# A new listed order of all steps for a fused decay attention and mixture-of-experts attention kernel

## The chip, the cores and the metric

The kernel runs on one core of one Trainium2 chip. The metric is the device time of one execution in microseconds (us); lower is better. Engines are named as the profile names them: PE is TensorE's matmul, PEld its weight load, DVE is VectorE, ACT is ScalarE, POOL is GpSimd, and SP is the queue from which all data transfers (DMAs) are issued.

## The reference

Two layers on a batch of 8, 576 positions, 8 heads of 64. The first is causal attention whose scores get a decay made from a running sum of log(f); the second is a mixture of 4 attention experts of 64 columns, of which each position takes the best 2.

```
scores = q @ k.T / 8 + cum[:, None] - cum[None, :]      # cum = cumsum(log(clip(f)))
attn   = softmax(causal(scores)) @ v                    # 8 batches, 8 heads
x      = attn, heads side by side                       # [8, 576, 512]
for e in range(4):
    ye  = softmax(causal((x @ wq[e]) @ (x @ wk[e]).T / 8)) @ (x @ wv[e]) @ wo[e]
    out += (e among the best 2 of x @ w_gate) * its weight * ye
```

## The kernel before

**Units.** The work is cut into 48 units of two heads (or two experts) each: `a0_0` to `a0_3` are the four pairs of heads of batch 0, `m0_0` and `m0_1` the two pairs of experts of batch 0, and so on. Each unit goes through the same tasks. `prep` loads or computes queries and keys and splits them into a rounded part and a rest (L386, L389, L401 on ACT, L399 on DVE, for three early units on POOL; L544 on PE for experts). `max` finds the row maxima: matmuls into PSUM (L618), reductions by DVE (L624, L640, L673, L680), a transpose on PE (L685), a copy on ACT (L688), and a small DMA into the key tile (L376). `scores` makes the scores (L716, L717 on PE) and their exponentials (L734 to L770 on ACT), and then lets POOL work: it cuts the diagonal blocks (L703, two at a time, 128 partitions; L772 for the last 64 rows, 64 partitions) and sums the probabilities by columns (L776, L778, L780 on 128 partitions, L782 on 64). `attend` multiplies by the values (L801). For each pair of units `rows` sums the rows on PE (L839), transposes the result on DVE (L854, twice), adds a constant (L857, 128x18 elements), takes the reciprocal (L859), spreads it (L865 on ACT, L868 on DVE) and sends it round by DMA (L874); `apply` scales the outputs with it (L886, L905, L913). Experts have a `front` as well (values and gate: L439, then many small DVE operations, L473 to L505, and L512) and an `out` (L936, L940, and the output DMAs, L943 and L946).

**What sets the order.** Each task is a Python generator that yields after every step of a few instructions. `ORDER` lists 4939 steps, two digits of base 64 for each: the task's number. Each time a number comes, that task goes on to its next yield. So `0a` is `rows a0_1`, `0f` is `scores a0_2`, `0k` is `scores a0_3`, `0q` is `max a1_0`, `0v` is `max a1_1`, `0t` is `prep a1_1`, and `4w` is the task that keeps PE warm with 110 matmuls on zeros (L205) during the start. At the end of the function every instruction is chained behind the one before it on its own engine, so each engine runs its instructions exactly in the listed order, and one that waits holds up all behind it on that engine. `SLOTS` says for each new tile which buffer it takes: three for the probabilities (`P`), eight PSUM banks (`banks`), five wide tiles, twenty strips, and so on. ORDER and SLOTS were written by a replay of the whole program outside the kernel, which is not part of the source.

Of the kernel before, what the change touches and what calls it, by code (L numbers as in the profile page):

```python
# [37 lines left out]
0C0C0C0C0F0v0k0v0F0F0r0r0w0w0w0w0r0l0w0m0m0s0m0w0w0b4A0m4A0m0b0C0m0b0w0m0b0w0w0w0b0b0H0H4y0b0A0w0w0w0m0H0H0m0C0C
0C0C0w0w0w0w0w0C0O0w0M0H0b0H0H0n0H0H0R0s0s0H0n0n4A0n0n0N0N0N0R0R0n0n0H0H0H0n0n0H0w0R0H0H0H0w0M0M0N0H0H0H0H0H0H0H
0H0N0N0R0N0N0N0N0A0N0A0w0M0M0Y0w0R0R0w0N0N0N0N0N0N0N0N0N0N0N0N0N0N0N0N0N0N0N0N0N0N0N0N0O0N0r0D0D0D0D0D0D0D0O0O0O  # L40
0O0O0D0D0r0r0r0D0D0D0D0H0H0O0O0O0O0D0D0u0F0D0D0D0O0O0H0H0O0O0O0O0O0O0O0M0Y0w0F0D0Y0O0F0Y0x0x0x0O0O0D0D4A0y0y0I0y
0O0O0y0y0O0Y0S0I0I0I0I0I0I0I0I0I0I0I0I0I0I0I0I0I0Y0I0y0O0N0N0+0R0n0+0+0+0+0+0+0D0D0D0D0D0y0R0R0I0I0+0+0+0O4A0O0O
# [40 lines left out]
323230302X2X2X2X2X2X2X2X2X30303030303030303030322C323232302X322S322C31312N2I2X2S2I2N2N2I2C3c2C2C2X2X2X2T2T2T2T2T
2T2T2T2T2T2T30323030302T2T322T2T2T2T2C32323232323032322C2C31312T2O2O2W3c2O322O3c353535352Y2Y2Y2Y2O2T2T3230322T32
2R2Y2Y2Y2Y2Y2Y2Y2Y2Y2Y2Y2Y3c3c3c352Y2Y2Y2Y323232322Y2O3c353535353d2C322C2O3h2T2T2T353535353535353535362T3535353e
3e3535353535353e3e3e3e3e3e3e35353535353535353535333333362U36362U2U2Y362Y2Y322Y2Y36363636363h363e2O2O333330303030
# [957 lines left out]
```

## Time and profile before

| | us |
|---|---|
| median of 3 runs | 648.0 |
| the three runs | 646.73, 648.0, 650.79 |
| the profiled execution | 649.53 |
| its span, first to last instruction | 647.8 |
| PE busy in the span | 632.1 |
| DVE busy | 554.8 |
| ACT busy | 480.0 |
| POOL busy | 408.3 |

The profiled execution took 1.7 us more than its span, and 1.5 us more than the median of the three runs. Matmuls overlap in the records, so that busy time on PE says that matmuls were under way, not how densely they followed each other.

### The profile page before, as it was taken

Reading aid. Unit: us, or ns where it says so; the run is one execution under the profiler, and the core shown is the slowest. Engines: PE = TensorE matmul, PEld = TensorE weight load, DVE = VectorE, ACT = ScalarE, POOL = GpSimd, SP = SyncE. Lnnn points to the kernel's source line nnn. Section 1 sums busy time; section 2 is a strip of 40 time slices with the busy share of each in tenths; the row PEclk is TensorE's granted clock in tenths of the full one; section 3 lists DMA queues with packets and bytes.
Section 4 is the critical chain, followed back from the end, with each engine's and each line's share of the span. In section 5 each row is a group of like instructions: output and inputs, shape, how many; then the busy total and the mean of one; then the engine's idle time right before and its main releaser. Section 6 shows DMA issues by size and latency. Waiting matters only on the chain.

```text
span 647.8 us, 15136 instructions
## 1 busy us (share of the span) xinstructions
PE 632.1 (98%) x5303; PEld 539.5 (83%) x5303; DVE 554.8 (86%) x1541; ACT 480.0 (74%) x1057; POOL 408.3 (63%) x519
## 2 busy tenths in 40 slices
...
GB/s 201 168 141 155 91 79 165 116 135 87 157 88 125 136 71 155 113 131 77 93 184 86 152 122 94 142 74 131 168 95 83 191 98 58 80 92 69 60 83 203
DMA packets 33531, 76.90 MB, mean 119 GB/s; under 512 B 4395, under 2 KB 4875, under 8 KB 33455
## 3 DMA queue, kind: packets, MB, share of 16 engines
...
q14 instruction: 34, 0.28, 0.1%
...
## 4 chain that ended last, share of the span: by engine, by line
PE 93%; DVE 4%; DMA 1%; issue 1%; ACT 0%; POOL 0%; ACTq 0%; DVEq 0%
PE pp_m L544 16%; PE ob_a L801 10%; PE s_a L717 7%; PE s_a L716 7%; PE m_a L618 7%; PE po L936 7%; PE pv L439 7%; PE ob_m L801 5%; PE m_m L618 4%; PE s_m L717 4%; PE s_m L716 4%; PE oa_a L801 4%; PE sm_a L839 3%; PE warm L205 2%; PE oa_m L801 2%; PE sm_m L839 1%
## 5 line engine op out<-in xcount | busy, mean ns | idle before, releaser
L703 POOL TENSOR_SCALAR_AFFINE_SELECT P_a<-P_a 128x256 f32<-128x256 f32 x128 | 65.7, 530 | 102.6 <-ACT P_a L734 61.7
L716 PE MATMUL s_a<-ka_a 128*128 128x320 f32 (+4 forms) x384 | 104.3, 296 | 0.0
L717 PE MATMUL s_a<-kq 128*128 128x320 f32 (+4 forms) x384 | 102.5, 294 | 1.6 <-DMA kq<-ms_a 1.6
L624 DVE CUSTOM_DVE_ANT_0 junk_a<-m_a,mask 128x192 bf16<-128x192 f32 (+2 forms) x186 | 86.8, 484 | 15.1 <-PE m_a L618 12.5
L618 PE MATMUL m_a<-kq 128*128 128x448 f32 (+3 forms) x372 | 78.6, 306 | 6.1 <-DVE mxs_a L624 4.8
L552 ACT ACTIVATE kq<-pp_m 64x288 fp32r<-64x288 f32 x128 | 51.7, 404 | 33.0 <-PE pp_m L544 31.7
L717 PEld LDWEIGHTS s_a<-kq 128*128 128x128 f32 (+1 forms) x384 | 68.6, 180 | 3.6 <-DMA kq<-ms_a 2.4
L716 PEld LDWEIGHTS s_a<-ka_a 128*128 128x128 f32 (+1 forms) x384 | 69.2, 180 | 2.9 <-issue 0.9
L557 DVE TENSOR_TENSOR ka_m<-pp_m,kq 64x288 fp32r<-64x288 f32 x128 | 58.2, 455 | 12.9 <-ACT kq L552 10.7
L776 POOL TENSOR_TENSOR R_a<-P_a 128x896 f32<-128x896 f32 x32 | 68.5, 2144 | 0.0
L801 PE MATMUL ob_a<-P_a,va 128*64 128x320 f32 (+1 forms) x512 | 68.5, 410 | 0.0
L618 PEld LDWEIGHTS m_a<-kq 128*128 128x128 f32 x372 | 57.6, 180 | 11.5 <-DVE mxs_a L624 6.2
L703 POOL TENSOR_SCALAR_AFFINE_SELECT P_m<-P_m 128x256 f32<-128x256 f32 x64 | 30.5, 492 | 56.8 <-ACT P_m L734 43.4
L801 PEld LDWEIGHTS ob_a<-P_a,va 128*64 128x64 f32 x512 | 36.3, 139 | 24.6 <-issue 1.0
L778 POOL TENSOR_TENSOR R_a<-R_a,P_a 128x640 f32<-128x640 f32 x32 | 53.9, 1685 | 1.6
L716 PE MATMUL s_m<-ka_m 128*128 128x192 f32 (+3 forms) x192 | 51.3, 293 | 0.0
L717 PE MATMUL s_m<-kq 128*128 128x192 f32 (+3 forms) x192 | 50.3, 294 | 0.0
L624 DVE CUSTOM_DVE_ANT_0 junk_m<-m_m,mask 128x448 bf16<-128x448 f32 (+2 forms) x96 | 44.9, 483 | 6.0 <-PE m_m L618 5.0
L399 DVE TENSOR_TENSOR ka_a<-xin_a,ka_a 64x1152 fp32r<-64x1152 f32 x32 | 46.6, 1457 | 0.9 <-ACT ka_a L389 0.2
L399 DVE TENSOR_TENSOR ka_a<-xin_a,kq 64x1152 fp32r<-64x1152 f32 x29 | 42.8, 1475 | 0.7
L734 ACT ACTIVATE P_a<-s_a 128x512 f32<-128x512 f32 x64 | 35.8, 595 | 5.8 <-PE s_a L717 5.5
L386 ACT ACTIVATE kq<-xin_a 64x1152 fp32r<-64x1152 f32 x32 | 37.1, 1158 | 3.5 <-DMA xin_a<-in_qk_dram 3.2
...
## 6 DMA issues: line engine op xcount, KB each, us to landing
...
```

Source lines behind the costliest of these rows:

```text
L399: eng.tensor_tensor(lo, x[at], hi.bitcast(F32), ALU.subtract)
L544: nc.tensor.matmul(pp[:, :HS], w[:, c, es], x[c][:, gs], start=(n == 0), stop=(n == 3 * KC - 1))
L552: nc.scalar.activation(hv[h], src[h], AF.Copy)
L557: nc.vector.tensor_tensor(lo[:, h, gs], src[h], hv[h].bitcast(F32), ALU.subtract)
L618: nc.tensor.matmul(dst, qB[0:K, h, i0 : i0 + dst.shape[0]], kB[0:K, h, j0:j1], start=True, stop=True)
L624: nc.vector.tensor_tensor_reduce(jk[:, :n], src, mask[:, MW - n :], 1.0, init, ALU.add, ALU.max, acc)
L703: return nc.gpsimd.affine_select(pv, pv, [[0, 2], [1, 128]], ALU.is_ge, 0.0, base=0, channel_multiplier=-1)
L716: nc.tensor.matmul(dst, kaf[:, c : c + m], qA[:, h, i0:i1], start=True, stop=False)
L717: nc.tensor.matmul(dst, kqf[0:K, c + h * S : c + h * S + m], qB[0:K, h, i0:i1], start=False, stop=True)
L776: g.tensor_tensor(r[:, :, 128:S], p[:, :, 320:768], p[:, :, 768:1216], ALU.add)
L778: g.tensor_tensor(r[:, :, 256:S], r[:, :, 256:S], p[:, :, 1216:1536], ALU.add)
L801: mm = nc.tensor.matmul(dst[64 * h : 64 * h + 64, c0 : c0 + rhs.shape[-1]], vs[h][0:kp, blk], rhs, start=first, stop=last,)
```

## The change

ORDER and SLOTS are replaced; no instruction is added, removed or altered. Both lists hold the same 4939 steps, each task as often as before, and give 4311 PE instructions, 1157 on DVE, 1055 on ACT, 514 on POOL and 378 DMAs, as before. (The profile counts some more: a matmul on plain fp32 is two there, and a reduction with an accumulator read is two.) The scores and the row sums of the units come in the same order as before; in `max` one pair of neighbours and in `attend` six pairs change places. There are 110 warming matmuls as before, of which some now stand a little later. The new lists come from a replay in which POOL's operations on 64 partitions can keep DVE off the shared port for a whole run of POOL operations. Of the 104 lines of ORDER and the changed lines of SLOTS these matter for the text: the lines around `rows a0_1` (the fourth `0a` is L857, the fifth L859) and, as a sample, the slots of the probabilities and wide tiles.

```diff
 ORDER = """
...
-0q0q0q0q0q0q0q0q0f0f0f080k0q0q0k0t0k080k0q0q0q0q0k0q030f0k0q0q0f0q0q080q0q0q0t0t0A0k0k0f0k0k0k0k0k0o0q0q0a0t090k
-0q0q0q0q0q0k0k0a0k0v0k0k0f0v0v0v0v0v0v0v0f4A0a0v0v0v0k0k0a0g0A0A0v0F0a0v0v0v0r0v0a0a0v0r0r0r0k0r0r0A0v0v0v0v0v0v
...
+0q0j0j0q0f0f0f0f0q0q0t0q0k0k0k0A0q0k0q0d0f0f0q0k0t0k0k0k0a0t0t0k0a0a0a0a0f0q0F040k0k0k0q0k0q0k0f0k0q0q0f0k0q0i0k
+0k0q0q4A0q0q0q0k0k0k0k0k0f0q0v0v0v0v0v0v0f0v0v0v0v0p0v0A0k0q0A0a0A0F0a0g0v0v0v0v0v0v4A0v0v0g0t0k0q0o0v0l0v0q0l0a
...
 SLOTS = """
-P 01201201201202102102102010210210201201210212012012
-wide 01234234102314023410231042230142104214302142032041320123012431243124013421304123041
...
+P 01201201201021021021012010210120120120102101201021
+wide 01234243120423102143021430123401324014320143014302143210324102410340213420314203142
...
```

## Rows read from the trace of the kernel before

**Rows 1.** The page: busy time by engine, share of the span, instructions
```profile
PE 632.1 (98%) x5303; PEld 539.5 (83%) x5303; DVE 554.8 (86%) x1541; ACT 480.0 (74%) x1057; POOL 408.3 (63%) x519
```

**Rows 2.** The page: the chain that ended last, by engine
```profile
PE 93%; DVE 4%; DMA 1%; issue 1%; ACT 0%; POOL 0%; ACTq 0%; DVEq 0%
```

**Rows 3.** Stretches: length, busy by engine (instructions), granted clock, DMA share, GB/s
```profile
0.00:20.00 20.00, 16.78 (x123) 13.34 (x124) 13.77 (x33) 15.49 (x19) 18.56 (x29) 1.00 0.65 213
...
40.00:60.00 20.00, 17.46 (x148) 13.68 (x146) 18.76 (x45) 15.29 (x31) 17.75 (x21) 1.00 0.51 140
...
400.00:500.00 100.00, 100.00 (x853) 85.89 (x855) 86.73 (x248) 77.59 (x173) 64.97 (x86) 1.00 0.46 120
```

**Rows 4.** Waits of PE: total us, times, longest us
```profile
PE m_a L618 <- DVE mxs_a L624: 4.8, 5, 2.8
PE mp_a L600 <- DVE mxs_a L597: 2.1, 2, 1.2
PE s_a L717 <- DMA kq<-ms_a: 1.6, 3, 0.8
...
PE m_a L618 <- DMA kq<-ex: 0.7, 1, 0.7
PE mp_a L685 <- DVE mxs_a L624: 0.7, 1, 0.7
```

**Rows 5.** Timeline of DVE, 54 to 61 us: start, length, instruction
```profile
54.86 5.05 DVE L857 TENSOR_SCALAR rc_a<-zt_a 128x18 f32<-128x18 f32 x1
```

**Rows 6.** Line 857: lengths as min/median/max ns
```profile
L857 DVE TENSOR_SCALAR rc_a<-zt_a x16: 160/178/5053, 54.9 to 573.6; 128x18 f32<-128x18 f32 x16
```

**Rows 7.** Timeline of POOL in the same stretch
```profile
54.35 0.76 POOL L703 TENSOR_SCALAR_AFFINE_SELECT P_a<-P_a 128x256 f32<-128x256 f32 x2
55.06 0.28 POOL L772 TENSOR_SCALAR_AFFINE_SELECT pl<-pl 64x128 f32<-64x128 f32 x1
55.33 1.56 POOL L778 TENSOR_TENSOR R_a<-R_a,P_a 128x640 f32<-128x640 f32 x1
56.85 2.08 POOL L776 TENSOR_TENSOR R_a<-P_a 128x896 f32<-128x896 f32 x1
58.89 0.98 POOL L780 TENSOR_TENSOR R_a<-R_a,P_a 128x384 f32<-128x384 f32 x1
```

**Rows 8.** Timeline of PE, 60.5 us on; in brackets its idle time before
```profile
60.58 0.41 PE L618 MATMUL m_a<-kq 128*128 128x320 f32 x1 [2.77 <-DVE mxs_a L624]
```

**Rows 9.** Chain that ended last: start us, us, what; 61 to 97 us
```profile
61.17 1.54 PE oa_a L801 x8
62.71 2.98 PE ob_a L801 x20
...
94.91 0.80 PE oa_a L801 x8
95.71 2.06 PE ob_a L801 x20
```

**Rows 10.** A stretch behind the wait, columns as in rows 3
```profile
62.00:64.00 2.00, 2.00 (x12) 1.22 (x10) 1.90 (x9) 1.73 (x4) 0.00 (x0) 0.50 0.48 93
```

**Rows 11.** Timelines of DVE and POOL: two other long DVE operations
```profile
154.42 2.13 DVE L857 TENSOR_SCALAR rc_m<-zt_m 128x18 f32<-128x18 f32 x1
...
151.16 5.36 POOL L776 TENSOR_TENSOR R_a<-P_a 128x896 f32<-128x896 f32 x2
156.48 1.57 POOL L778 TENSOR_TENSOR R_a<-R_a,P_a 128x640 f32<-128x640 f32 x1
...
182.95 3.21 DVE L473 TENSOR_TENSOR g<-vm 128x80 f32<-128x80 f32 x1
...
181.24 0.29 POOL L772 TENSOR_SCALAR_AFFINE_SELECT pl<-pl 64x128 f32<-64x128 f32 x1
181.50 2.10 POOL L776 TENSOR_TENSOR R_a<-P_a 128x896 f32<-128x896 f32 x1
...
184.52 1.54 POOL L778 TENSOR_TENSOR R_a<-R_a,P_a 128x640 f32<-128x640 f32 x1
```

More of the change, by code (lines that the diff above doesn't have):

```diff
@@ L38 @@
[L38 to L42, printed above, removed]
@@ L83 @@
[L83 to L86, printed above, removed]
-33333333333333333333333333333333363e2D3636362P363e3e3e363636332D2D332P363636362T3h2D363e2Z353e3e363e3e3e3636363c
@@ new lines @@
+4w4w4w4w4w4w4w4w4w4w4w4A4x050000000500000202020202020c02020207024w024w4w4w4w4w0207074z02020202060202020202024A4A
+020c4w020202020207074w4w4w4w054w4w4w074z0c024w03034w070707074w054w0702020707074y0707074w4w4w4w070c0c0c0c03030707
+034w050303030e03070h03030303034z030303030707074z4z074z4z0303030303070707070e0e0e0h0e0e0e0e0e0e0h0j040e0e0c0c0e0e
+0e0e0e0e4z0e080303080h080e0e0e080808080h08080808080h08080h0e080e0e0j0j0j0o0t040e0j0j0j0e0e080808080808084w4w080e
+0j0j0o0o0j0j0j0j0j0j0j0j0j0j0j0j0j0j0j0j0e0j0o0h0f0f0f0f0o0f0f0o0o0q0f09080j0t0j090f0f080f0f0f0f03080q0A0q0f0q0q
@@ new lines @@
+0r0n0H0H0b0A0M0H0N0N0R0R0A0Y0N0N0N0N0u0M0N0N0N0N0N0N0N0N0N0N0N0N0N0N0N0N0N0N0N0N0N0N0N0O0N0D0M0D0R0D0D0O0O0O0D0N
+0r0O0O0r0O0M0M0O0O0D0D0D0D0O0D0N0H0D0D0O0O0D0D0O0D0D0D0O0O0G0F0O0O0O0D0H0H0O0w0r0w0D0H0F0F0x0H0N0D0D0D0Y0x0O4y0y
+0b0+0y0M4A0I0Y0Y0Y0Y0I0I0I0O0O0N0O0M0M0O0I0I0I0I0O0I0I0I0I0I0I0I0I0I0y0I0I0I0I0I0I0I0y0y0y0R0Y0O0O0O0O0R0R0R0R0R
+0R0R0R0R0R0R110R0D0R0R0R0R0R0M0R0R0R0R0R0R0R0R0R0R0P0P0P0P0M0M0D0R0S0S0+0+0+0+0+0S0S0S0+0P0P0M0P0R0S0S0S0+0P0S0P
+0P0P0P0S0+0S0y0P0Z0M0M0M0M0M0S0S0S0S0S0I0I0D0P0P0P0S0S0P0S0S0S0S0P0P0P0y0P0+0+0M0M0M0M0M0S0D0S0S0M11110M0M0M0+0+
@@ new lines @@
+0+0+0+0+0+0+180+0+0+0R0S0S180+0+11110S0+0K0z0K0z0K0J0K0K0M0M0M0S0S0Y0M0M0+0E0E0M0J0J0x0+0E0y0P0P0P0P0T0+0z1d130M
+0z0M0M0M0T0T0T0T0T0T0T0T0T0T0+11111313130+13130T0T0T130T0T131313130T1a0T0Q13130T0T0T1313131813130-0-0T130T0T180K
+0-0-1313131813130Q0Q0T0-0-0-0-0-0-0-13130P0K0-190-0K0-0-0-0-1a0z0z0z1a1a0T0M1a1a1a1a1a1a0K1k0-0-0-0-0z131313131d
+1a110U0U0U180L0L180-100z1a0L1d4A4A1a1a1a1a1a0L140L0L14141a1a1k140L181a14141f1a1a1a1a1a0M1l1l0M0M140L141a0M1l0M14
+14141l141a140L141m0V0M0M1a100M0M141k141d1d1d141f14140V1k141a1a1k1b141p0V1f1b1b1k1f0V0V1f1f1f0V1f1f1b1b1b1l1l1l1l
@@ new lines @@
+101l1l1f1b1f1l1l14141414141l1l1l1l1b1l1b1b1b1b1b1b1l1w1l1b1d1f4A1f4A1l1l0-0-0-1f1f1f1f1f1l1l1l1f1f1f1f1f0-1l1l1l
+1f1f1l1l1l1l1b1b0V1l1l1l1l1l1p1p1f1p4A1p1k1k4y1m1d1b1f1m1m1m1m1m1m1m1m121f0z0z0V1k1f0L0L1f1e1m1p1p1p1p1p1p1p1p1p
+1p1p1p1p1p1p1p1b1b1b1b1b1p1p1b4A1p1p1p1p1p1p1p1p1p1p1l1g1p1m1m1m1m1m1p1p1b1g1q0V0V1g1m1m1m1g1m16161g1q161q1q1q1g
+1g1g1k1l1m1k1k1p1q1q1q1q1q161q1k1k1g1g1g1g1g1g1g161g1g1m161q1w1q1q1q1k1k1k1q1q0W1m1m1m1B1q1q1q1q1q1q1q1g1g1g1g1q
+0W161w1w1w1g1B1q1w1w1w1b151c0W0W161g1m1c1h0W0W0W0W1m1m1m1m1q1q1k1k1k1k1p1k151y1c1517171g1y1y1h1k1k1k1k1k1y1y1y1y
@@ new lines @@
+1y1y1y1k1k1k1n1g1n1n1n1n1n1g1n1y1n1n1n1n1y1h1y1y1y1n1n1n1n1n1y1y1y1y1n1n1i1B1n171k1q1r1i1i1i1n1n1q1k1I1r1N1r1r1k
+1n1k1k1k1k1k1k1B1r1r1r1r1r1r1r1r1r1r1r1r1r1r1r1r1r1r1r1I1n1o1i1i1B1B1B0W1y1y1I1I1B1I1D0X1y1y1D1D1D1D1D1D1D1D1D1D
+0X1y1716170X0X1y0X0X1y1N0X0X0X1i171o1D1o1D1D1D1D1D1D1D0X1D1y1K1n0X0X1D1D1y1D1D1D1K1y1D1y171i171s1s1k1D1n1n1D1r1K
+1K1K1z1z4y1z1z1K1K1D1K1K1K1K1D1z1P1z1z1z1z1z1z1j1z1i1K1s1z1z1K1K1K1K1K1K1K1k1j1k0X1k1k1z1r1z1r1z1E1j1z1N1V1K1E1N
+1k1E1E1j1j1j1j1E171k1E0X1t1K1K1t1N1t1j1k1j1U1K1I1E1E1E1E1E1E1E1E1E1V1V1E1U1K1K1K1U1U1U240W1U0X1E1E1K1V1I1N1N1V1K
@@ new lines @@
+1z1z1V1z1V1z1I1V1V1V1E1K1j1V1K1V1V1k1E1E1E1k1z1j1V1E1P1V1P1P1P1V1V1V1V1V1V1V1V1V1E1V1V1V1V1V1V1V1V1V1V1L1L1L1L1L
+1L1N1C1P1Z1U1P1P1P1P1U1U1P1U1U1L1L1L1L1L1W1E1E1P1P1P1t1P1P1L1L1P1P1P1L1L1L1z1L1W1P1L1W1t1z1Z1t1P1P1P1z1L1L1L1L1Z
+1Z1Z1t1t1t1t1L1Z1W1J1Z1Z1Z1L1Z1L1W1W1W1W1W1W1L1U1Z1P1P1P171V1W1Z1Z1Z1Z1Z1V1Z1Z1Z1Z1Z1Z1Z1Z1Z1Z1Z1Z1Z171Z1Z1Z1Z1Z
+1x1V1W1W0W2g1Z241P1P1G1G1G1G1F1G1Z1A1G1W1G1P1A1u1P1u1F1G1u1O1+1u1A1Q1Q1Z1Q1Q1Q1Q1u1+1Z1u1u1W1W1U1Q1Q1Q1Q1U1Q1Q1Q
+1Q1H1Q1Q1+1u1W1W1+1+1Q1U1W1+1Q1Q1W1Q1Q1+1+1Q1Q1Q1Q1+1+1U1U1U1U1U1U1U1U1+1W1F1+1W1W1W1W1W1G29291+1+1+1v1+1+1+1+1V
@@ new lines @@
+241+1+1W1W1+1+24241+1+1M24241M1u1u1u1+1H1R1R1U1W1H241W1Q1S1S1S1S1R1+1+1+1H26262626261X1X1X261S1+1X1X261X1S1H1H1v
+1H1H1v1v26261U1M251S1X2b1U1U26261U1U1X1U1U1U1X1X1X1X2626261X1X1X1U1U2h1S1U1X1X26262626261H262626261S1X1X2626261v
+1-1-1-1-1v1v1U1X291v1U1T1U1U2g1X1-1-1v1X1-1-1v1-1-1-1-1-1-1-2929291-1-1-1-1-1Y2g261T1-262b2b29291Y1Y2l1-1v2g2g2b
+1T1T1T1T2s2s1T1T2b2l2b2b2i2b2b2b202b1-1T1-1-2i2i2026262s2b1U2i2b271v27272i1X271H1U1U1-2727272b2b2b2b2b2b2i2b2i1v
+1v2i2b2b2s272i27272i1X1X1v1v1v2s2i1v271X2727272i1U2b2b2i2i2i272i2b2b2i1v27272i2i272b2b1U1U2l2i2i2a2i2b212b1U1U1U
@@ new lines @@
+2s2s2s2s2727272s2s2c2n2i2c1U2c2c2c2c2c2c2l2l2l2s2c2c2c2c2t2t2t2t2c2s2s2s2c2c1v2c2c2n2c2t212g2c2c2121212n212i2c2l
+212c2c2n2n2n2n2n2n27272n2n2l2i212c2c21212s2s2s2t2t2t2t2t2t2t2t2t2t2t2t2t2t2t2t2t2t2t2t2t2t2t2t2t2t2t2i2n2n2n2s27
+2t2t2n2s2n272x2n2n2n202n2c1H2i271v2s2i222n2u2n2n2n2n2n222222222828281T2d2d2t2i2i2g2t2g2m2e2n2222222e2e2e1T2s2u2u
+2n2e2s2E2s2j2j2j2j2j2j2u2u2J2n2u2u2u2s2u2u2u2e2j2s2s2s2s2j2j2j2j2j2j2j2s2e2u2d222s2u2s2n2u2u2u2u2u2o2o2o2o2o2o2j
+2e2j2u2j2j2u2j2u2u2u2u2E2s2E2o2j2o2u2o2u2o2o2o2s2s2o2o2f2f2j2j2E2E2o2o2o2o2E2u2Q2s2s2s2u2f2s2s2o2o2o2s2o2x2s2t2E
@@ new lines @@
+2u2x2x2x2x2o2o2o2o2x2x2x2x2x2x2x2x2x2x2x2x2x2x2x2x2x2x2x2x2x2x2x2x2x2x2x2x2x2x2f2f2f2t222G2G2G2e2G2G2G2k2k2y2y2y
+2x2x2y2y2y2y2y2y2G2G2G2y2y2k2u2p2G2s2p2j2G2y2y2j2j2y2y2y2y2y2J2E2y2v2y2y2v2v2v2j2y2v2v2y2y2y2v2v2v2v2v2v2y2v2v2G
+2v2v2v2v2v2v2v2v2v2v2v2s2s2v2R2G2y2G2y2G2G2G2G2G2G2G2G2y2y2q2G2q2w2G2q2J2q2q2w2q2G2Q2s2q2z2G2J2z2z2z2z2z2z2z2z2z
+2z2z2z2z2z2J2L2z2z2L2q2w2z2z2z2z2G2J2G2f2f2L2J2G2z2z2z2z2G232L2L232L2p2L232323232323232q2L2L2L2L2Q2z232H2L2L2L2L
+2L2L2H2L2L2H2H2L2H2Q2H2r2L232L2V2r2r2H2H2H2H2H2H2H2r2L2L2L2L2r2H2H2r2r2H2H2H2f2A2B2r2r2B2H2f2f2K2H2s2J2L2A2A2L2Q
@@ new lines @@
+2s2S302L2B302Q2Q2B2B2s2B302V2V30232H30302S2S2S3030302S2S2S232H2M2M2M2H2H2X30232S2L232S2S2S2V2M2M2M2F2H2V2M2M2S2S
+2S2S2S302M2M2S2S2S2S2S2S2B2B30302M302Q3h2M2S2S2M2M2M2M2M30302X302S2B2S2X2X2X312X2X2X2M2S2S2X2M2S31312X3131312V35
+302V312X2V31313131313c3130312M2M3131313131223030312M2M2C2T2T2X302M2M2M312S312X31322r2r2X2T2H312X2X2X313131313131
+322X31312X31302T2X2X2T2X2T2T2X2X2X322T30302T2X3132303032322T303030302T2T2T2B2T3032313230302C303030302T2C302T3232
+2T2X2T3c312X3c2X302I302C2C302C31312N2O2C322T2N2I322O2T2T322X2I323e32323232322Y323c2Y2O32322Y2Y2Y2Y2T2T2T2Y2O2Y35
@@ new lines @@
+3c2Y2Y32324y3e323e352Y2Y2Y2Y2Y3e322Y2Y2O2O3e3e2Y2Y2Y2Y2Y2Y2Y32323c2C4y3235353c353535353535352Y353535352Y35353535
+35353535353535353532353h2T3e3e353e3e35352O2N3e332O2U35353o352C2C303333332C30303e3e333e2U3c36363636363636362U2D36
+2O3e333333333e3333362D362D35333333332T36353636363636363e3e3e3333362W36332D333333333336303e3e3e3e3h3h3h36363e3636
+2P2+302Z303e3e30363636363h2Z363t2P3o34343e37372+2+2+2+2+3e2P2P3j343e3737373737373737373737373737373e3j3h3p2+2+2+
+2P373o3o373j3j3j3j33333j33372Z2P2D2D2D2D2D37373j3j3q3j3f373f3f3f3f3f3f3f3f3f3f3f3j2-2P3j3j3j3j3j3j2-3j3j3j3j383o
@@ new lines @@
+0X3j2-3j3j3j3h3q3q2P3f3q383q2-3q3q3q3q3j3q3q3f3f2P3f3f3f2D2D3q3q3i383737373f2-2P3B2-3q3q3q3q3q3q3q3f3f393j2-3t3B
+3t3j3B3q2-3B3q3q3A3A3A2-3A3j3A2D3j3k3k3k3k3k3k3k3k3k3k3k3k3k3k3k3t3t2-3o3t3o3k3A3A3A3q3A3A3v3v3q3A3v3v3v393q3k3f
+3f3v3k3q3o3B3k3k3k3B3k3B3B3k3v3v3A3A3C3F3F3F3q2P393q3q3B3B3B3B3B3B3B3B3B3B3B3B3v39393v3B3B3B3B3B3B3B3B3B3B3B3B3B
+3B3B393r3B3B3C3r3r2-3B3r3C3r3k3A3A3A3C3C3C3C3C3C2D3C3f3A3v3r3r3r3r3r3F3C3r3r3r3r3r3C3A3v3v3v3v3r3r3v3M3C3A233d3A
+3C3C3C3C3v3v3k3f3f3v3C3C3r3r3k3C3v3r3r3A3t3r3r3r3v3r3v3v3F3F3F3F3F3v3A3A3A3v3939393C3C3C3A3A3A3A3v3F3F3F3F3C3F3F
@@ new lines @@
+3F3F3F3F393F3F3F3F3F3F3F3F3F3F3F3F3F3v3r3F3m3F3A3A3A3A3A3A3a3m3l3v3v3v3a3Y3m3F3a3g3a3F3C3C3C3a3a3F3m3t3M3C3C3C3G
+3G3g3G3G3G3G3G3G3G3A3G3G3m3l3l3A3a3w3w3w3w3w3w3w3w3w3w3w3w3w3w3w3w3w3G3G3R3A3A3a3A3G3G3G3G3G3G3A3A3G3w3G3w3T3w3w
+3w3w3F3M3R3w3m3M3M3G3G3G3G3A3M3G3D3D2D2D2D3D3D3g3s3s3s3M3G3u3D3A3A3D3D3D3G3D3D3D3D3D3G3G3a3D3D3D3w3D3O3O3O3O3O3O
+3O3O3m3O3O3D3x3w3y3y3R3x3D3D3O3y3b3O3R3R3D3b3D3D3D3D3x3R3H3H3H3H3O3O3b3m3O3O3H3y3T3T3T3H3H3T3T3D3H3H3T3T3b3H3T3y
+3T3T3H3n3H3H3H3O3O3H3O3H3H3H3H3O3H3H3H3O3O3O413O3O3b3T3Y3Y3O3T3T3b2D3T3T3T3T3T2D3y3b2D2D3T3O3T3T3m3T3T3O3O3O3n41
@@ new lines @@
+3A3y3y3Y3Y3Y3Y3M3A3I3T3H3H3H3H3T3Y3R3E3E3E3n3R3I3J3J3A3T3b3T3T3P3P3P3P3P3P3I3A3P3P3P3S3z3z3+3+3+3+3+3+3+3+3b3+3+
+3+3N483P3P3J3b3b3z3+3y3+3b3n3+3P3P3P3P3P3P3+3n3+3n3n3U3U3U3+3+3+3+3P3P3+3P3P3P3+3+3+3T3J3J3b3b4a3+413n3b3U3U3z3U
+3U3U3U3U3U3U413U3U3U3n3U413A413z3U3U3U3U3U3Q3J3+3+3z43433z3z3z3z3+3+3P43433+3P3P3b3P3Q484843434343433n3Q3U433J3J
+4949494949494349484849493J49494949414949494949494949494949493-3-493-3-4d4343434949494949494949434d4d433n3-3-433U
+3U3U3-3-3-3-3-3-3-43433-3-3a3-484a4343433K48484848434a434d3U4d3J433-3K3K4a4949414a4a4d3K3-4d434343434a433K4d4d4d
```

100 lines of the change are left out of this document (20 added, 80 removed).

## The prediction

> **What bounds the kernel now.** I read the page first: PE is busy for 632.1 of 647.8 us, far ahead of DVE [rows 1], and the chain that ended last runs through PE for 93% of the span, DVE for 4% [rows 2]. An order of steps cannot make PE's 5303 matmuls fewer, so all that it can win is time in which PE stands still or runs slowly. The second view cuts the span into stretches [rows 3]. From 400 to 500 us PE is busy all of the time, and the reader should take from this that the steady state has almost nothing left. The idle time lies at the start: 3.2 us in the first 20, and 2.5 us from 40 to 60. The third view says what PE waited for [rows 4]: DVE's reductions 4.8 us in all, of which one wait is 2.8, and four smaller causes, which with those five waits come to 9.9 us.
>
> The one long wait has a history that the timelines tell. At 54.86 us DVE reaches L857, an operation on 128x18 elements, and needs 5.05 us for it [rows 5]; the median of that line is 178 ns [rows 6]. In these 5 us POOL runs five operations with no gap: the second L703, which ends at 55.11, then L772, L778, L776 and L780, until 59.87 [rows 7]. L857 ends at 59.91, as soon as the run is over. Behind it on DVE stand the reductions of `max a1_1`, and for these a matmul waits that holds up PE's queue for 2.77 us [rows 8]. The still PE then loses its clock: at 62 to 64 us the granted clock is 0.50, the lower of the two levels, 1.2 GHz instead of 2.4 [rows 10]. One `attend` takes 1.54 + 2.98 us there, and 0.80 + 2.06 at 94.91 us, at the full clock [rows 9].
>
> **The change part by part.** *The hold at L857.* With it gone PE saves the wait of 2.77 us and the slow clock, (1.54 - 0.80) + (2.98 - 2.06) = 1.66 us: 4.4 us together. Does the new list take it away? In the old one, GpSimd's L776 of a0_2 and the second pair of L703 of a0_3 stand ahead of L857 and L772 of a0_3 behind; POOL came to that L772 0.2 us after DVE came to L857 [rows 5, 7]. In the new one, L857 follows both L854 at once; ahead of it on POOL stand the second pair of L703 of a0_2 and the first of a0_3, and behind it L772 of a0_2, which needs ACT's L770, listed after L859. So POOL should have nothing ready but L703s when L857 arrives. I take -4.4 us, with a chance for the opposite below; the bounds are -4.4 and, if the same hold comes back longer, a loss (first rival).
>
> *Which runs hold.* Not every run of POOL does it. At 154.42 us an L857 came as one L776 was followed by another, both on 128 partitions, and got through when the second ended, after 2.13 us, though an L778 followed at once [rows 11]. At 182.95 an L473 waited 3.21 us through L776, L780 and L778, and that run began with L772, on 64 partitions [rows 11]; so did the run at 55.06 from the point where L857 could have gone [rows 7]. Three cases are few, but they agree with what the new replay supposes, so that it should see such runs where the old one did not. The Trainium skill, SBUF — State Buffer, section on the two separate sides, says that the port pair which VectorE and GpSimd share is locked for one whole instruction, and that the other engine waits for that one. By that rule L857 would have gone at 55.11, after 0.25 us, and there would have been nothing here to win; the trace, with 5.05 us through four further instructions, does not agree.
>
> *The other holds.* Those at 154.42 and 182.95 cost DVE 2.0 and about 3 us, and no long wait of PE names them: the other four waits for the reductions come to 2.0 us [rows 4], and PE has other work listed meanwhile. I take -0.5 us for all of them, between 0 and -2.0.
>
> *The start.* The first unit's chain (load, split, maxima, transpose, row of maxima by DMA) sets the first 30 us, and the warming matmuls only fill it. In the new list a reduction of a0_1 stands between the two heads' reductions of a0_0, and two value loads have moved from just ahead of the load of a0_3's extra rows, one before it and one behind; L399 of a0_1 on POOL comes after two more weight splits, and on DVE after three more reductions. The waits of this stretch are 2.1 us for L597, 1.6 and 0.7 us for DMAs and 0.7 us for the first transpose [rows 4]. The first two sit in the unit's own chain, which the list does not shorten; the last two may shrink. I take -1.0 us, between -3.0 and +2.0 (a L399 that comes late for the scores of a0_1 would be the loss).
>
> *Everything else* (six pairs of `attend` that change places, hundreds of small shifts) lies in a stretch where PE never waits. I counted in ORDER and SLOTS how much PE work lies between the last write to a PSUM bank and its next owner: under 1.5 us in 68 of 1009 cases before, 96 in the new list, and only two are new at the bottom (0.6 us). With 68 of them PE was still busy for 100.00 of 100 us [rows 3], so I take nothing for that. The last 26 us of PE's list are the same but for a few matmuls of L936 that changed places. Each list has collisions that its replay does not see; outside the long hold the waits of PE come to 9.9 - 2.8 = 7.1 us [rows 4], nearly all in the start. For new ones of this sort I put +1.0 us, between 0 and +4.0.
>
> *Sum*, against the profiled execution: 649.5 - 4.4 - 0.5 - 1.0 + 1.0 = 644.6 us. That execution was 1.5 us above the median of the three runs, which spread over 4 us, so part of the hold may be milder in them; I take 0.6 off for the median and forecast 644.0 us, with a range of its own from 640 to 648.
>
> **The rivals.** *The hold comes back at its new place (slower).* L772 of a0_2 needs L770, and ACT's list puts that after L734 and L744 of a0_3; DVE has an L399 and both L854 to do before L857. If ACT is through first, L857 meets L772, L776, two L703, L772, L776, L778 and L780 with no gap: 0.28 + 2.08 + 0.76 + 0.28 + 2.08 + 1.56 + 0.98 = 8.0 us by the lengths of rows 7. The old hold left 4.8 us after its L703 and gave 2.8 us of idle PE, so PE had cover for 2.0 us; now 6.0 us would be idle, and with 1.7 us of slow clock the loss is 7.7 in place of 4.4, which is 649.5 + 3.3 = 652.8 us. The point from which it decides is whether L772 starts before L854 has ended. For it speaks that in the old run POOL was far ahead of its place in the list; against it, that this is the very case the new replay models.
>
> *The collisions only move (no change).* One hold out of 24 L857 and about a hundred small operations of the fronts cost PE much; a list with other timings may have another one elsewhere, or the start may lose what the hold gives. Then the time is 649.5 - 4.4 + 4.4, or 647 to 651 us. The change not doing what it says belongs here too: the replay's rule may avoid holds that never cost PE anything.
>
> *More than the hold.* If the new start also hides most of its 5.1 us of waits, and the DVE holds vanish: 649.5 - 4.4 - 2.0 - 4.0 = 639 us.
>
> **How the numbers follow.** The forecast gets 0.50, the hold at the new place 0.15, the moved collisions 0.22, and the large gain 0.13. A measurement of this kernel tells 1% (6.5 us) from no change, hardly less. Faster by over 1%, under 641.5 us: the large gain and the low end of the forecast, 0.13 + 0.12 = 0.25. Slower by over 1%, over 654.5 us: the upper half of the first rival and a bad end of the second, 0.10. Within 1%: 0.65. The range from 638.5 to 653 leaves out about half of the large gain, the upper part of the first rival and a little of the second, together 0.2.
>
> **What would show it.** In the changed profile L857 of `rows a0_1` should take about 0.18 us, PE should show no wait over 1.5 us behind it, and the clock should stay at 1.00 from 56 to 66 us. The stretch from 400 to 500 us should stay at 100. An L857 of several us behind an L772 would be the first rival; a long wait of PE somewhere else, with another line of DVE next to it, the second. The prediction is wrong if the steady state itself moves by more than 3 us, since I give it nothing.

## The result and the profile after

The new list takes 642.88 us (median of 20 executions, 640.84 to 650.62), the old one beside it on the same chip 649.73 us (20 executions, 646.73 to 652.34): the medians are 6.9 us apart. The ratio of the means is 0.9912, with a 95% interval of 0.9889 to 0.9935: 0.9% faster, 5.7 us. It leaves out the execution of 650.62 us, which counts as slow, and it lies nearer to 1 than the ratio of the medians because seven executions of the new list took over 645 us. The ratios below are of means too. The profiled execution took 642.41 us with a span of 640.7.

The page of the new list answers to [rows 1, 2]: the same work on PE, 4.9 us less busy time, and DVE 13.7 us less: the same operations, which now spend less time waiting inside their own records, as L857 did.

```profile
PE 627.2 (98%) x5303; PEld 538.1 (84%) x5303; DVE 541.1 (84%) x1541; ACT 481.9 (75%) x1057; POOL 409.7 (64%) x519
...
PE 88%; DVE 6%; issue 2%; DMA 2%; ACT 1%; SPq 1%; POOL 0%; DVEq 0%; POOLq 0%
```

Stretches of the new list, columns as in [rows 3]. From 40 to 60 us PE is busy for 19.75 us in place of 17.46, and the clock that was 0.50 in [rows 10] stays at 1.00. The first 20 us did not improve, and two stretches that lay in the steady state now have holes: 276 to 284 us, and something of 1 us between 400 and 500.

```profile
0.00:20.00 20.00, 16.31 (x119) 12.97 (x119) 14.15 (x35) 15.47 (x19) 18.23 (x30) 1.00 0.59 192
40.00:60.00 20.00, 19.75 (x170) 14.79 (x169) 18.24 (x53) 19.58 (x36) 18.93 (x22) 1.00 0.66 186
56.00:66.00 10.00, 10.00 (x91) 7.87 (x89) 9.69 (x34) 8.87 (x20) 9.88 (x15) 1.00 0.43 113
276.00:284.00 8.00, 5.80 (x48) 4.26 (x47) 7.96 (x17) 4.67 (x11) 7.47 (x7) 1.00 0.10 36
400.00:500.00 100.00, 98.95 (x837) 84.92 (x836) 87.22 (x241) 73.85 (x168) 65.33 (x81) 1.00 0.45 119
```

What PE waited for, as in [rows 4]: no wait is over 1.2 us.

```profile
PE m_a L618 <- DVE mxs_a L624: 3.1, 4, 1.1
PE mp_a L600 <- DVE mxs_a L597: 1.5, 2, 0.9
```

The place of the hold, timelines of DVE and of POOL as in [rows 5, 7]. L857 takes 0.23 us. It starts at 50.54, as soon as the two L854 are through, and L772 starts at 50.70: the step got past by less than 0.2 us.

```profile
49.67 0.83 DVE L854 STREAM_TRANSPOSE zt_a<-sm_a 128x288 f32<-128x288 f32 x2
50.54 0.23 DVE L857 TENSOR_SCALAR rc_a<-zt_a 128x18 f32<-128x18 f32 x1
...
49.28 1.47 POOL L703 TENSOR_SCALAR_AFFINE_SELECT P_a<-P_a 128x256 f32<-128x256 f32 x3 [0.74 <-ACT P_a L765]
50.70 0.29 POOL L772 TENSOR_SCALAR_AFFINE_SELECT pl<-pl 64x128 f32<-64x128 f32 x1
50.96 2.11 POOL L776 TENSOR_TENSOR R_a<-P_a 128x896 f32<-128x896 f32 x1
```

**Where the time went.** Busy time cannot show this, since overlapping matmuls are busy in any case. So I gave every matmul the median length of its line and size, without what overlaps its neighbour, summed these lengths in the order of each list, and read in both traces when PE had come to the same sum. The difference is PE's lead over the kernel before (us, negative is ahead). The columns are the sum in us; PE comes to 50 at 64 us in the new list, to 250 at 269, to 270 at 293 and to 410 at 439. The lower rows belong to experiments below. A column that falls into a wait or a slow stretch changes by about 1 us with the way in which the lengths are taken.

```
                                   40    50    80   170   210    250   270   400   410   600
new list                         -0.1  -4.7  -6.8  -7.5 -10.2  -10.3  -7.1  -7.8  -6.2  -7.0
new list, L772 on 128            -0.6  -4.9  -6.9  -7.7 -10.3  -10.2  -7.0  -7.8  -7.7  -9.2
new list, L782 on 128 (646.99)   -0.6  -5.2  -7.3  -8.0 -10.6  -10.6  -7.4  -8.2  -2.4  -2.4
old list, L772 on 128            -0.2  -5.0  -5.0  -5.1  -6.8   -6.9  -6.8  -6.8  -6.8  -6.8
```

The new list is level at the start, wins 4.7 us at the hold, wins 5.6 more up to 269 us, loses 3.2 from there to 293 and 1.6 at about 435, and ends 7.0 us ahead (two small gains of 0.7 and 0.8 us, from 270 to 400 and from 410 to 600 of the sum, make up the rest). The losses stand in the timelines. At 274 to 283 us three of DVE's operations of `apply`, normally 0.75 us, each wait for one POOL operation that is in the way (L776, L778, L776), and PE waits 1.06 and 1.14 us behind them, in this order on DVE and PE:

```profile
274.57 2.54 DVE L913 TENSOR_TENSOR xl_a<-ot_a,xh_a 128x576 fp32r<-128x576 f32 x1
277.04 2.09 DVE L886 TENSOR_TENSOR ot_a<-bt_a,ot_a 128x576 f32<-128x576 f32 x1
...
280.53 2.15 DVE L913 TENSOR_TENSOR xl_a<-ot_a,xh_a 128x576 fp32r<-128x576 f32 x1
...
280.66 0.39 PE L618 MATMUL m_a<-kq 128*128 128x256 f32 x1 [1.06 <-DVE mxs_a L624]
283.42 0.80 PE L618 MATMUL m_a<-kq 128*128 128x448 f32 x5 [1.14 <-DVE mxs_a L624]
```

At 430 us two L886 take 3.83 us together; the second comes while an L772 runs. This place turns out to matter most (the runs on L782 and L772 below).

```profile
430.15 3.83 DVE L886 TENSOR_TENSOR ot_a<-bt_a,ot_a 128x576 f32<-128x576 f32 x2 [0.47 <-DMA bt_a<-rr_a]
...
430.47 0.72 POOL L772 TENSOR_SCALAR_AFFINE_SELECT pl<-pl 64x128 f32<-64x128 f32 x1
431.14 0.09 POOL L614 MEMSET mxs_a<- 64x2 f32 x1
431.21 2.10 POOL L776 TENSOR_TENSOR R_m<-P_m 128x896 f32<-128x896 f32 x1
433.26 1.35 POOL L703 TENSOR_SCALAR_AFFINE_SELECT P_a<-P_a 128x256 f32<-128x256 f32 x2
```

### The profile page after: what moved, and what is told of

Its sections match the earlier page's. It is cut to its first block, busy times and chain, and to the rows that moved or that the text cites. A ratio compares the mean times of both kernels' runs of the same rounds, so it can differ in the third digit from the quotient of the medians.

```text
span 640.7 us, 15170 instructions
## 1 busy us (share of the span) xinstructions
PE 627.2 (98%) x5303; PEld 538.1 (84%) x5303; DVE 541.1 (84%) x1541; ACT 481.9 (75%) x1057; POOL 409.7 (64%) x519
## 4 chain that ended last, share of the span: by engine, by line
PE 88%; DVE 6%; issue 2%; DMA 2%; ACT 1%; SPq 1%; POOL 0%; DVEq 0%; POOLq 0%
PE pp_m L544 16%; PE ob_a L801 10%; PE pv L439 7%; PE po L936 7%; PE s_a L716 7%; PE s_a L717 7%; PE m_a L618 6%; PE m_m L618 4%; PE ob_m L801 4%; PE oa_a L801 4%; PE s_m L716 4%; PE s_m L717 4%; PE sm_a L839 3%; PE warm L205 2%; PE oa_m L801 1%
## 5 line engine op out<-in xcount | busy, mean ns | idle before, releaser
L703 POOL TENSOR_SCALAR_AFFINE_SELECT P_a<-P_a 128x256 f32<-128x256 f32 x128 | 65.3, 527 | 112.7 <-ACT P_a L734 67.2
L618 PE MATMUL m_a<-kq 128*128 128x448 f32 (+3 forms) x372 | 80.7, 304 | 4.0 <-DVE mxs_a L624 3.1
L776 POOL TENSOR_TENSOR R_a<-P_a 128x896 f32<-128x896 f32 x32 | 67.5, 2110 | 0.1
L618 PEld LDWEIGHTS m_a<-kq 128*128 128x128 f32 (+1 forms) x372 | 57.6, 180 | 9.7 <-DVE mxs_a L624 4.4
L703 POOL TENSOR_SCALAR_AFFINE_SELECT P_m<-P_m 128x256 f32<-128x256 f32 x64 | 33.7, 543 | 48.2 <-ACT P_m L734 31.0
L778 POOL TENSOR_TENSOR R_a<-R_a,P_a 128x640 f32<-128x640 f32 x32 | 55.3, 1731 | 1.8
L716 PE MATMUL s_m<-ka_m 128*128 128x192 f32 (+2 forms) x192 | 51.8, 295 | 0.0
L717 PE MATMUL s_m<-kq 128*128 128x192 f32 (+2 forms) x192 | 50.9, 294 | 0.0
L624 DVE CUSTOM_DVE_ANT_0 junk_m<-m_m,mask 128x192 bf16<-128x192 f32 (+2 forms) x96 | 44.9, 485 | 5.3 <-PE m_m L618 4.3
L399 DVE TENSOR_TENSOR ka_a<-xin_a,ka_a 64x1152 fp32r<-64x1152 f32 x32 | 47.9, 1497 | 0.7
L399 DVE TENSOR_TENSOR ka_a<-xin_a,kq 64x1152 fp32r<-64x1152 f32 x29 | 42.5, 1465 | 0.8
L618 PE MATMUL m_m<-kq 128*128 128x320 f32 (+3 forms) x192 | 41.2, 298 | 0.0
```

The lines of the kernel that those rows point to most:

```text
L399: eng.tensor_tensor(lo, x[at], hi.bitcast(F32), ALU.subtract)
L618: nc.tensor.matmul(dst, qB[0:K, h, i0 : i0 + dst.shape[0]], kB[0:K, h, j0:j1], start=True, stop=True)
L624: nc.vector.tensor_tensor_reduce(jk[:, :n], src, mask[:, MW - n :], 1.0, init, ALU.add, ALU.max, acc)
L703: return nc.gpsimd.affine_select(pv, pv, [[0, 2], [1, 128]], ALU.is_ge, 0.0, base=0, channel_multiplier=-1)
L716: nc.tensor.matmul(dst, kaf[:, c : c + m], qA[:, h, i0:i1], start=True, stop=False)
L717: nc.tensor.matmul(dst, kqf[0:K, c + h * S : c + h * S + m], qB[0:K, h, i0:i1], start=False, stop=True)
```

## The experiments

Theory: runs of POOL operations that hold an operation on 64 partitions keep DVE off until the first gap; the new list wins by moving L857 out of one. Rivals: a hold lasts one POOL instruction, as elsewhere, and L857 met something else; or the gain is in the list's other parts.

**Only the four steps moved, in the old list.** L857, L859, L865 and L868 of `rows a0_1` stand behind the last reduction of `max a1_1`; all else as before.

```diff
-0v0v0v0k0k0a0g0A0A0v0F0a0v0v0v0r0v0a0a0v0r0r0r0k0r0r0A0v0v0v0v0v0v0v0v0f0l0g0g0l0k
+0v0v0v0k0k0g0A0A0v0F0v0v0v0r0v0v0r0r0r0k0r0r0A0v0v0v0v0v0v0v0v0a0a0a0a0f0l0g0g0l0k
```

> The old list with one change: the four steps L857, L859, L865 and L868 of rows a0_1 stand behind the last reduction of max a1_1 instead of among them. If the hold at L857 is what cost PE its 2.77 us and its clock, L857 now comes to its port at about 58 us and waits 2 us at most, with nothing urgent behind it: PE shows no wait over 1.5 us between 50 and 66 us, and the time falls by 4.4 us (644 to 646 us against 649.7); by up to 7 if the waits at 78 and 81 us were DVE's backlog from it. If the gain of the new list is spread over the whole layout and the hold is a small part, it falls by 2 us or less.

646.93 us (12 executions, 645.14 to 651.52), ratio 0.9961 with an interval of 0.9941 to 0.9981; the kernel before had 649.88 in the same session. The hold is gone, L857 takes 0.64 us, and no wait of PE is over 1.5 us, but only 2.9 us are won, between what the two sides of the expectation asked for. The late `rows` work has a price: ACT stands still for 2.06 us until L859 lets L865 go, all that is listed behind L865 on ACT comes later, and PE waits 1.37 us at 64.25 for one of these, the copy of a row of maxima (L688).

```profile
59.14 0.64 DVE L857 TENSOR_SCALAR rc_a<-zt_a 128x18 f32<-128x18 f32 x1
...
60.11 0.68 ACT L865 ACTIVATE zt_a<-rc_a 128x576 f32<-128x576 f32 x1 [2.06 <-DVE rc_a L859]
...
64.25 0.42 PE L716 MATMUL s_a<-ka_a 128*128 128x320 f32 x1 [1.37 <-ACT ms_a L688]
```

**The hold put back, in the new list.** L857 and L859 stand behind L776 of a0_2 again.

```diff
-0a0t0t0k0a0a0a0a0f0q0F040k0k0k0q0k0q0k0f0k0q0q0f0k0q
+0a0t0t0k0a0a0f0q0F040k0k0k0q0k0q0k0f0k0q0q0f0a0a0k0q
```

> The new list with L857 and L859 of rows a0_1 moved back by two reductions, behind L776 of a0_2, so that L857 comes at about 52 us while L776 (51.0 to 53.0) runs, which follows the 64-partition L772. If a 64-partition operation lets the whole gapless run of POOL hold the port, L857 is held until about 57.5 us, over 5 us, and PE loses 4 to 7 us: 647 to 650 us against 642.9. If the port is held for one instruction only, L857 waits until 53.0 us, 1.2 us, which PE's cover of 2 us takes up: 642.5 to 643.5 us.

649.61 us (12 executions), ratio 0.9999, interval 0.9978 to 1.0021. These two steps undo the whole change, by a hold that is larger than the old one. L857 comes in the middle of L776 and waits through six more operations, until the run ends at 57.06 and POOL rests for the first time; PE stands still for 4.96 us (2.77 in [rows 8]).

```profile
51.34 5.75 DVE L857 TENSOR_SCALAR rc_a<-zt_a 128x18 f32<-128x18 f32 x1
...
50.16 0.28 POOL L772 TENSOR_SCALAR_AFFINE_SELECT pl<-pl 64x128 f32<-64x128 f32 x1
50.42 2.11 POOL L776 TENSOR_TENSOR R_a<-P_a 128x896 f32<-128x896 f32 x1
52.50 0.76 POOL L703 TENSOR_SCALAR_AFFINE_SELECT P_a<-P_a 128x256 f32<-128x256 f32 x2
53.22 0.28 POOL L772 TENSOR_SCALAR_AFFINE_SELECT pl<-pl 64x128 f32<-64x128 f32 x1
53.48 2.06 POOL L776 TENSOR_TENSOR R_a<-P_a 128x896 f32<-128x896 f32 x1
55.50 1.52 POOL L778 TENSOR_TENSOR R_a<-R_a,P_a 128x640 f32<-128x640 f32 x1
56.97 0.09 POOL L614 MEMSET mxs_a<- 64x2 f32 x1
...
58.09 4.11 PE L801 MATMUL ob_a<-P_a,va 128*64 128x320 f32 x16 [4.96 <-DVE mx_a L673]
```

**The 64 partitions taken away, in the old list.** No step moves; L772 works on all 128 partitions of its tile, of which the upper 64 hold zeros.

```diff
-            p4[:64], p4[:64], [[0, 2], [1, 64]], ALU.is_ge, 0.0, base=0, channel_multiplier=-1
+            p4, p4, [[0, 2], [1, 64]], ALU.is_ge, 0.0, base=0, channel_multiplier=-1
```

> The old list, with L772 on 128 partitions instead of 64 (rows 64 to 127 of that tile are zeros and stay zeros; the result is the same). If a 64-partition operation is what lets a run hold the port, L857 of rows a0_1 gets in at the next seam of the run, within 0.5 us, L473 at 183 us within 1 us, and the time falls by 4 to 7 us (643 to 646 us against 649.7). If any gapless run of POOL holds the port, nothing changes: L857 takes about 5 us and the time stays at 649 to 650.

643.45 us (6 executions, 642.57 to 645.09), ratio 0.9902, interval 0.9879 to 0.9926. L857 stands where it stood, POOL runs the same five operations without a gap [rows 7], and L857 gets in between the first two of them:

```profile
54.65 0.28 DVE L857 TENSOR_SCALAR rc_a<-zt_a 128x18 f32<-128x18 f32 x1
...
54.12 0.77 POOL L703 TENSOR_SCALAR_AFFINE_SELECT P_a<-P_a 128x256 f32<-128x256 f32 x2
54.84 0.30 POOL L772 TENSOR_SCALAR_AFFINE_SELECT pl<-pl 128x128 f32<-128x128 f32 x1
55.09 1.58 POOL L778 TENSOR_TENSOR R_a<-R_a,P_a 128x640 f32<-128x640 f32 x1
```

This is the clean separation at L857: same order, same run of POOL, no hold. The version wins 6.4 us, which the lead table splits into 4.8 us at the old hold and 1.7 between 189 and 232 us. Only the 4.8 us are shown to come from the hold; the 1.7 are taken up in the part on why the prediction was right.

**How many partitions.** As before, with `p4[:96]` in both places.

> The old list with L772 on 96 partitions of its tile in place of 64 (rows 64 to 95 are zeros and stay so). Theory one: what lets a run of POOL operations keep DVE off is an operation that stays within the first 64 partitions; then 96 do as well as 128, L857 near 54.8 us takes at most 0.3 us, and the time is 643 us (the 128-partition form gave 643.45). Theory two: it is any operation on fewer than 128 partitions; then L857 takes 5 us again, PE waits 2.8 us at 60.6 us, and the time is 649 us.

649.62 us (10 executions), ratio 0.9993, interval 0.9975 to 1.0012. Theory two: 96 partitions hold DVE just as 64 do, and PE waits 2.76 us at 60.31 us.

```profile
54.60 5.04 DVE L857 TENSOR_SCALAR rc_a<-zt_a 128x18 f32<-128x18 f32 x1
...
54.79 0.29 POOL L772 TENSOR_SCALAR_AFFINE_SELECT pl<-pl 96x128 f32<-96x128 f32 x1
```

**Both lists without these operations.** L772 as above, and L782, the other one on 64 partitions in each unit:

```diff
-        u["summed"] = g.tensor_tensor(r[0:64, :, 512:S], r[0:64, :, 512:S], p4[:64], ALU.add)
+        u["summed"] = g.tensor_tensor(r[:, :, 512:S], r[:, :, 512:S], p4, ALU.add)
```

The new list with both edits:

> The new list, with L772 and L782 both on 128 partitions (the added rows are zeros; the result is the same). If 64-partition operations make the long holds, none is left: no small DVE operation over 2.2 us, the runs of the new kernel that came to 645 to 650 us with a clock of 0.988 to 0.997 are gone, and the median is 641 to 642.5 us against 642.9. If they don't matter, median and spread stay as they are (642.9, seven of twenty runs over 645).

639.98 us (6 executions, 638.86 to 641.44), ratio 0.9848, interval 0.9823 to 0.9873. The old list with both edits:

> The old list with L772 and L782 on 128 partitions, the same two edits that took the new list to 639.98 us. Theory one: the new list gains by more than the holds that begin with operations on 64 partitions (between 60 and 170 us its PE gets ahead by 2.7 us, which L772 on 128 partitions in the old list did not give). Then the old list stays 2 to 4 us behind the new one with the same edits: 642 to 643.5 us. Theory two: the holds are all that the new list avoids; then without them both lists take the same time, 640 us.

644.7 us (6 executions, 643.47 to 645.47), ratio 0.9917, interval 0.9901 to 0.9934. The new list with L772 alone:

> The new list with L772 alone on 128 partitions, L782 on 64 as before. Theory one: L772 ahead of L776 makes the holds, so that this edit brings all of the 2.9 us: 640 us and no run over 643. Theory two: L782 at the end of each unit's sums also starts runs that hold DVE; then this version lies between, 641 to 642 us.

640.02 us (4 executions, 639.71 to 641.07), ratio 0.9852, interval 0.9835 to 0.9869. So L782 is out of it: with or without its edit the new list takes 640.0, and the old one takes no less with it (644.7, and 643.45 without). The 1.25 us that it takes more go with a wait of PE of 0.89 us at 209.31 us, which the profile with both edits has and the one with L772 alone has not (the L496 below). Theory one held in all three, but its times were off: for the new list with both edits it had 641 to 642.5 us, 1 us too high, and for the old one 642 to 643.5, 1 us too low. The four versions of list and L772 together:

```
              L772 on 64    L772 on 128
old list        649.9         643.45
new list        642.9         640.0
```

Without the holds behind L772 the new list is still 3.4 us better, or 4.7 with L782 widened in both lists. So of the 6.9 us of the change, between a third and a half is what it avoids of these holds. The new list with L772 on 128 partitions beats the change by 2.9 us.

**The new list's executions above 645 us.** Seven of its 20 took 645.45 to 650.62, the other 13 at most 643.33. The mean granted clock was 0.988 to 0.997 in the seven and 0.999 to 1.000 in the 13, so that each of the seven had some stretch at the lower level. The first guess was my own first rival, a lost race of L857 against L772. Here ACT's L770 of a0_2 is moved behind two L750, so that L772 comes later:

```diff
-0k0a0a0a0a0f0q0F040k0k0k0q0k0q0k0f
+0k0a0a0a0a0q0F040k0k0k0q0k0f0q0k0f
```

> The new list with one step moved: ACT's L770 of a0_2 stands behind the two L750 of a0_3 instead of ahead of them, so that L772 of a0_2 starts about 1 us later (51.7 us in place of 50.70) and L857 of rows a0_1, which reaches DVE at 50.54, has over 1 us of room in place of 0.2. Theory one: in the executions of the new list that took 645 to 650 us (7 of 20) L772 came ahead of L857 and the hold came back. Then these vanish here: the best runs stay at 641 to 643 us, none is over 645, the median is 642 us, ratio to the kernel before 0.988. Theory two: these executions lose their time in other places (the DVE operations held at 274 to 284 and at 431 us). Then a third of the runs stays above 645 us and the median at 643 us.

643.19 us (9 executions, 642.1 to 649.17), ratio 0.9915, interval 0.9888 to 0.9943. L857 now comes 1.3 us ahead of L772 (0.26 us from 49.80, L772 at 51.09), and yet two of nine took 647.57 and 649.17. Theory one fell. The next guess was L399 behind L782; L782 alone on 128 partitions, L772 on 64:

> The new list with L782 alone on 128 partitions, L772 on 64 as in the change. The executions at 645 to 650 us came in 7 of 20 runs of the new list and in 2 of 9 with L770 moved. Theory one: what is lost in them is a run that begins with L772 (at L857 near 50.5 us, or later); then a quarter to a third of these runs stays above 645 us, and the best are at 641 to 642.5. Theory two: it is L399 of the early units, which reaches DVE at 48.16, 0.02 us after the second of two L782 on 64 partitions has given way to L703; where it comes a little earlier it waits through L782, the L703s and what follows. Then no run is above 645 us here.

642.8 us (6 executions, 641.87 to 648.79), ratio 0.9906, interval 0.9869 to 0.9942. Two were above 645 again, so L399 is not it, and the profiled one of 646.99 us was among them. Its L857 takes 0.23 us. The time is lost at 430 us (the lead falls from 8.2 to 2.4 us there): the first L886 waits for a DMA, comes at 430.11, and L772 has started at 430.09. Held until L778 ends at 434.71, the two L886 take 6.69 us in place of 3.83; PE waits 2.18 us behind them and then runs at the lower clock, 0.50 from 440 to 444 us.

```profile
430.11 6.69 DVE L886 TENSOR_TENSOR ot_a<-bt_a,ot_a 128x576 f32<-128x576 f32 x2 [0.79 <-DMA bt_a<-rr_a]
...
430.09 0.29 POOL L772 TENSOR_SCALAR_AFFINE_SELECT pl<-pl 64x128 f32<-64x128 f32 x1
430.33 0.09 POOL L614 MEMSET mxs_a<- 64x2 f32 x1
430.39 2.10 POOL L776 TENSOR_TENSOR R_m<-P_m 128x896 f32<-128x896 f32 x1
432.45 0.76 POOL L703 TENSOR_SCALAR_AFFINE_SELECT P_a<-P_a 128x256 f32<-128x256 f32 x2
433.18 1.53 POOL L778 TENSOR_TENSOR R_m<-R_m,P_m 128x640 f32<-128x640 f32 x1
...
437.26 1.48 PE L618 MATMUL m_a<-kq 128*128 128x192 f32 x5 [2.18 <-DVE mxs_a L624]
```

Its stretch from 440 to 444 us, columns as in [rows 3]:

```profile
440.00:444.00 4.00, 3.54 (x12) 3.03 (x13) 2.83 (x11) 2.91 (x8) 0.80 (x1) 0.50 0.03 9
```

In the version with L772 alone on 128 partitions the same two L886 take 1.55 us, where the new list's own profile had 3.83, and none of the ten executions of the new list with that edit was above 641.44:

```profile
430.25 1.55 DVE L886 TENSOR_TENSOR ot_a<-bt_a,ot_a 128x576 f32<-128x576 f32 x2 [0.54 <-DMA bt_a<-rr_a]
...
430.48 0.72 POOL L772 TENSOR_SCALAR_AFFINE_SELECT pl<-pl 128x128 f32<-128x128 f32 x1
```

**The new list unchanged, for more profiles.**

> The new list unchanged, for one more profile: of 20 executions 7 took 645 to 650 us, and no profile shows one. If this one falls among them, theory one expects L857 of rows a0_1 near 50.5 us to take over 5 us behind an L772, theory two L399 at 48 us to take over 4 us behind L782, a third that both are short and a wait of PE of over 3 us stands in another place. If it takes 641 to 643 us it says nothing on this.

> As the run before: the new list unchanged, for a profile of an execution at 645 to 650 us, with the same three theories.

> As the two runs before: the new list unchanged, for a profile of an execution at 645 to 650 us, with the same three theories.

643.43, 642.35 and 642.58 us: none was above 645. In all three L857 takes 0.23 us, and the second L886 near 432 us is held as in the profile above (3.0 us in each). The one of 643.43 us shows a second place where executions differ: it has the same two waits at 280 and 283 us as the new list's first profile (0.90 and 1.13 us), but behind them its clock falls to 0.50, where the first profile stays at 1.00, and its lead behind that place is about 1 us smaller. Its stretch, columns as in [rows 3]:

```profile
284.00:286.00 2.00, 2.00 (x8) 1.74 (x8) 1.92 (x10) 0.00 (x0) 1.92 (x2) 0.50 0.00 0
```

## Why the prediction was right, and where only by balance

The forecast of 644.0 us and its range hold the measured 642.88, but the parts of the sum fared differently.

- **The hold at L857, -4.4 us: right.** The lead grows by 4.7 us there, L857 takes 0.23 us, no wait of PE follows it up to 66 us, and the clock stays at 1.00 from 56 to 66 us. Putting the two steps back takes all of it away, though by a larger hold (4.96 us of idle PE in place of 2.77).
- **Which runs hold: right, and now shown.** Three cases in one trace suggested that a POOL operation on fewer than 128 partitions makes the difference; the three runs with 64, 96 and 128 partitions show it. The rule that I cited from the Trainium skill, SBUF — State Buffer (section on the two separate sides), that the other engine waits for one whole instruction, agrees with the trace where L772 has 128 partitions (0.28 us), and does not where it has 64 or 96 (5.05 and 5.04 us).
- **The other holds, -0.5 us, and everything else, nothing: too small.** From the end of the hold to 269 us the new list gains 5.6. A part of that the prediction could have read: it placed the other waits "nearly all in the start" and spoke of "a stretch where PE never waits", from the row of 400 to 500 us. In the old trace PE waits 0.49, 0.43, 0.41 and 0.89 us at 78.67, 81.08, 195.61 and 214.52 us; the new list has no wait over 0.3 us between 60 and 280 us. The first two stay with L772 on 128 partitions.

  Some 1.7 us lie between 189 and 232 us, where the old list with L772 on 128 partitions gains as much, but they are not the price of the held L473 [rows 11]. With L772 on 96 partitions L473 is still held, 2.82 us, and yet PE does not wait between 186 and 226 us and the gain is there as well. With L772 and L782 on 128 partitions L473 is free, and PE waits 0.89 us as in the old trace. What the two traces with this wait share is an L496 that comes just behind the start of an L778 and waits for this one operation, on 128 partitions: a collision that goes with the timing and not with L772. The old list, then the one with both edits, then the one with 96 partitions:

```profile
209.92 1.57 DVE L496 TENSOR_TENSOR gt<-gt,wins 128x20 f32<-128x20 f32 x1
...
209.90 1.54 POOL L778 TENSOR_TENSOR R_m<-R_m,P_m 128x640 f32<-128x640 f32 x1
...
214.52 0.38 PE L618 MATMUL m_a<-kq 128*128 128x256 f32 x1 [0.89 <-DVE mxs_a L624]
```

```profile
204.71 1.57 DVE L496 TENSOR_TENSOR gt<-gt,wins 128x20 f32<-128x20 f32 x1
...
209.31 0.38 PE L618 MATMUL m_a<-kq 128*128 128x256 f32 x1 [0.89 <-DVE mxs_a L624]
```

```profile
182.49 2.82 DVE L473 TENSOR_TENSOR g<-vm 128x80 f32<-128x80 f32 x1
```

  The remaining 3 us or so are left, by subtraction alone, for the list itself, which I had priced at nothing because PE is busy for nearly all of such a stretch. That was the wrong reading: a PE that is busy in this view can still do less in it, since overlapping matmuls hide how densely they follow each other, and only a comparison at equal work shows it. Which of the many small shifts give it was not tried.
- **The start, -1.0 us: not there.** At a sum of 40 us both are level (-0.1).
- **New collisions, +1.0 within 0 to +4: too small.** They cost 3.2 us at 269 to 293 us and 1.6 at about 435, in the profiled execution, and 3.8 more in the one execution above 645 us that a profile shows (6.2 against 2.4 us of lead).
- **First rival, the hold at the new place.** Its condition was right and close, 0.2 us. But it was not seen in any profile, and giving it more room did not remove the executions above 645 us. What did come was the second rival in kind: a hold behind L772, at another line and in the steady state. It is decided by which comes first, L772 or an L886 that a DMA's landing lets go: L772 by 0.02 us in the profile with the loss, L886 by 0.3 to 0.4 us in the four of the unchanged list.
- **"Wrong if the steady state moves by more than 3 us."** It did move, by 5.6 us one way and 4.8 the other, and the stretch from 400 to 500 us, which was to stay at 100, has 98.95. By its own sign the prediction was wrong about the steady state. The two terms that were both too small nearly cancel, and against the old list of the same session the gain is 6.9 us (5.7 by the means) where the sum had 4.9. The 0.6 us taken off for the median had no ground: over 20 executions the old list's median is 649.73 us, no lower than the profiled 649.53. The total is right for the hold, and by balance for the rest.

Open: whether all seven executions above 645 us lost their time at 430 us. One was seen, with another edit in it that moves no time. None of the ten executions with L772 on 128 partitions was that long, so that a hold behind L772 has a part in them; but the longest of the seven has a mean clock of 0.988 against 0.995 in the one seen, and so was at the lower level for more than twice as long.
